# An RWKV layer with two mixtures of experts: lone slots by column parts, the ranking in three portions, the last tiles' routing reordered

## The chip, the core and the metric

One core of one Trainium2 chip runs the whole kernel in one launch. The metric is the device time of one execution in microseconds (us), lower is better. A run counts with its own time. The profile belongs to one execution, and its times count from that execution's first instruction.

## The reference

Three stages follow each other: a linear attention with a decaying state, a first mixture whose eight experts all see all 1536 rows, and a second mixture that sends each row to one expert.

```python
# attention: B, H, S, D = 2, 8, 768, 48
for t in range(S):
    cur = einsum('bhd,bhe->bhde', u * k[t], v[t])
    y[t] = einsum('bhd,bhde->bhe', r[t], state + cur)
    state = w[t][..., None] * state + einsum('bhd,bhe->bhde', k[t], v[t])
x = y as 1536 rows of 384
# first mixture: 8 experts, 384 -> 1024 -> 384, all rows
P = 8 rounds of row and column scaling of exp(x @ w_gate - max)
x = sum over e of P[:, e] * (relu(x @ w1[e]) @ w2[e])
# second mixture: top 1
logits = normed(x) @ normed(expert_emb).T / tau
idx = argmax(logits); gate = softmax(logits)[idx]
out[row] = gate[row] * (relu(x[row] @ w1[idx]) @ w2[idx])
```

## The kernel before

The rows are 12 tiles of 128. TensorE does nearly all the work in products that take each operand as a high and a low part (three matmuls for one product), and the order of the whole program is written out by hand: a unit of work is a list of pieces, `run` issues a piece and then the side items that stand at its place in a second list. An engine executes its instructions in that order.

The last expert of the first mixture runs in four units of three tiles (`m1_unit(E - 1, ...)`). A unit has 8 hidden pieces (`h_piece`, L274, one per 128 hidden columns) and then the output pieces (`y_part`, L294 to L296), after which VectorE adds the tile to `acc` (`m1_finish`, L804). Beside the units run the steps of the second mixture's routing for tiles that are ready: `route_dots` (products with the embeddings, two thirds on VectorE at L731, one third on GpSimd at L738 and ScalarE at L724), `route_arg` (the choice), `gate_a` (an inverse norm, 13 small instructions on VectorE or 16 on GpSimd, L817 to L832), `route_pos` and `route_cum` (the row's place among its expert's rows), `gate_b`, `gate_c` (the softmax weight, L988), and `route_rows`, a scatter by GpSimd of each row to its place in the buffer `xs` (L958). Tiles 10 and 11 take `route_tr` and `route_mm` in place of the dots: three transposes (L893) and twelve small matmuls.

After the counts of the first tiles `choose` picks the expert that slot 0 will run, and after 8 tiles `order` ranks the other seven by their counts (23 small VectorE instructions, L1012 to L1049): slots 3, 5 and 7 (`TURN`, the lone slots) get the three smallest.

The second mixture is a sequence of ten slots (`m2_slot`). A slot loads its up to 256 rows from `xs` (`m2_load`, on SyncE's queue, behind all scatters so far), transposes and splits them (`m2_xT`, L707 to L712: TensorE, ScalarE, VectorE), and runs one expert. The expert's weights arrive in seven pieces in six stage buffers; each is split into a high part by ScalarE (L252) and a low part by VectorE (L258), which then lets SyncE load the next. Slot 0 computes both halves of 128 rows, a later slot its second half only under `tc.If`, by a bit of a word that is computed in slot 1.

A normal slot has 8 hidden pieces for 256 rows at once and 2 output pieces for each half. A lone slot works on one half (`turned_pieces` with `own=True`): three slabs accumulate x times the 1024 hidden columns in three PSUM banks, with the rows stationary; then ScalarE takes the relu of each bank (`hid`, L335); three `turn` steps transpose it into a bank of their own (L341), ScalarE writes the high part `hh` (L344) and VectorE the low part `hl` (L345); then come four output pieces. Its list has ten pieces: slab, slab, slab, turn, turn, turn, y, y, y, y.

Where side items stand is a table of numbers in `m2_slot`:

```python
if turned:
    its = its[KD:]
    at_ = (0, 1, 3, 5)
...
else:
    at_ = (5, 6, 7, 8, 9, 15, 15) if s == 0 else (1, 4, 6, KF, KF, KF + 1, KF + 1)
```

PSUM has eight banks, and `ps()` hands them out in turn. GpSimd's queue carries its arithmetic, the scatters and the output scatters in one order; SyncE's carries all loads in one order.

Of the kernel before, what the change touches and what calls it, by code (L numbers as in the profile page):

```python
# [19 lines left out]
def rwkv_sinkhorn_moe_top1_moe(  # L20
# [974 lines left out]
    def choose():  # L995
# [9 lines left out]
        nc.vector.tensor_scalar(oe, wdesc, m, None, op0=ALU.is_equal)  # L1005

    def order():
# [8 lines left out]
        nc.vector.tensor_scalar(mk, kio, est[:, 0:1], full, op0=ALU.is_ge, op1=ALU.mult)  # L1016
        b = small[0].tile([128, NS], F32, tag="b", name="b")
        nc.vector.tensor_tensor(b, kio, mk, ALU.add)
        nc.vector.tensor_scalar(ids[:, E - 1:E], est[:, 0:1], 0.0, None, op0=ALU.add)
        nf = sp.tile([128, E], F32, tag="fl", name="nf")  # L1020
        nc.vector.tensor_scalar(nf[:, 0:1], full, -1.0, 1.0, op0=ALU.mult, op1=ALU.add)
# [5 lines left out]
        key = sp.tile([128, E], F32, tag="jk", name="key")
        nc.vector.scalar_tensor_tensor(out=key, in0=p, scalar=float(E), in1=wdesc, op0=ALU.mult, op1=ALU.add)
        nc.vector.scalar_tensor_tensor(out=key, in0=oe, scalar=float(OOB), in1=key, op0=ALU.mult, op1=ALU.add)
        sq = [128, E, E]  # L1030
        c = sp.tile([128, NTILE, E], F32, tag="tmp", name="rank")[:, 0:E]
        nc.vector.tensor_tensor(
            c, key.unsqueeze(1).to_broadcast(sq), key.unsqueeze(2).to_broadcast(sq), ALU.is_gt
        )
        nc.vector.tensor_reduce(f, c, axis=AX.X, op=ALU.add)
        se = [128, E - 1, E]
        d = c[:, 0:E - 1]
        c = sp.tile([128, NTILE, E], F32, tag="tl", name="at")[:, 0:E - 1]
        nc.vector.tensor_tensor(
            c, f.unsqueeze(1).to_broadcast(se), want.unsqueeze(2).to_broadcast(se), ALU.is_equal  # L1040
        )
        nc.vector.tensor_tensor(d, c, wdesc.unsqueeze(1).to_broadcast(se), ALU.mult)
        nc.vector.tensor_reduce(b[:, 1:E], d, axis=AX.X, op=ALU.add)
        nc.vector.tensor_scalar(b[:, 1:E], b[:, 1:E], -1.0, float(E), op0=ALU.mult, op1=ALU.add)
# [495 lines left out]
```

## Time and profile before

| | |
|---|---|
| time, median of 3 runs | 1045.87 us (1043.79 to 1046.72) |
| the profiled execution's own time | 1045.61 us |
| its span, first to last instruction | 1043.9 us |
| PE (matmul) busy | 1015.2 us, 97% |
| DVE, ACT, POOL busy | 700.9, 413.9, 207.1 us |
| mean granted TensorE clock | 0.993 of full |
| moved by DMA | 91.71 MB, 85.60 MB of it through SyncE's queue |

PE is TensorE's matmuls, DVE is VectorE, ACT is ScalarE, POOL is GpSimd and SP is SyncE. The first mixture's last expert runs from about 780 us to 870, slot 0 from 870 to 892.6, the three lone slots from 928.0, 957.6 and 987.2, and the last matmul stands at 1034.1. A row of a timeline has the start, the duration, the engine, the line, the operation, what it writes and reads, and, in brackets, how long the engine had been idle and what ended that. Matmuls overlap, so the spacing of their starts tells how fast they go.

### The profile page before, as it was taken

Reading aid. Unit: us, or ns where it says so; the run is one execution under the profiler, and the core shown is the slowest. Engines: PE = TensorE matmul, PEld = TensorE weight load, DVE = VectorE, ACT = ScalarE, POOL = GpSimd, SP = SyncE. Lnnn points to the kernel's source line nnn. Section 1 sums busy time; section 2 is a strip of 40 time slices with the busy share of each in tenths; the row PEclk is TensorE's granted clock in tenths of the full one; section 3 lists DMA queues with packets and bytes.
Section 4 is the critical chain, followed back from the end, with each engine's and each line's share of the span. In section 5 each row is a group of like instructions: output and inputs, shape, how many; then the busy total and the mean of one; then the engine's idle time right before and its main releaser. Section 6 shows DMA issues by size and latency. Waiting matters only on the chain.

```text
span 1043.9 us, 19767 instructions
## 1 busy us (share of the span) xinstructions
PE 1015.2 (97%) x7714; PEld 995.0 (95%) x7714; DVE 700.9 (67%) x1413; ACT 413.9 (40%) x851; POOL 207.1 (20%) x393
## 2 busy tenths in 40 slices
PE   7999999999999999999999999999999998999996
PEld 6899999999999999999999999999999997999996
DVE  7998858666655665566456556655547787977764
ACT  3323234535432342333234323433434545566553
POOL 3211152040100010002001000000234663144101
PEclk9999999999999999999999999999999999999998
DMA  8435201201220122021011100120011314888762
GB/s 248 120 109 158 84 10 46 76 1 31 84 78 1 61 84 77 10 88 50 7 31 61 31 1 31 61 77 15 19 59 37 100 38 139 293 300 281 244 207 68
DMA packets 55783, 91.71 MB, mean 88 GB/s; under 512 B 5355, under 2 KB 47191, under 8 KB 55554
## 3 DMA queue, kind: packets, MB, share of 16 engines
q1 hardware_dynamic: 53056, 85.60, 26.4%
q0 software_dynamic: 2624, 4.75, 1.2%
q8 instruction: 64, 1.05, 0.4%
q14 instruction: 37, 0.30, 0.1%
q10 hardware_dynamic: 2, 0.00, 0.0%
HBM read 80.42 MB, written 13.28 MB: 90 GB/s over the span
## 4 chain that ended last, share of the span: by engine, by line
PE 67%; issue 14%; DVE 9%; POOL 5%; ACT 2%; DMA 1%; POOLq 0%; DVEq 0%; SPq 0%; ACTq 0%
PE ps L502 29%; PE ps L427 24%; PE ps L274 6%; PE ps L294 2%; PE ps L296 2%; PE ps L295 1%; POOL tmp L738 1%; DVE ps L731 1%; POOL xs L1136 1%; PE ps L631 1%; POOL out_dram L1182 1%; DVE hl L443 1%; DVE keep L438 1%; PE ps L663 1%; ACT hh L442 1%
## 5 line engine op out<-in xcount | busy, mean ns | idle before, releaser
L502 PE MATMUL ps<-wA,hh 128*128 128x384 f32 x864 | 221.6, 337 | 0.4 <-ACT hh L442 0.4
L502 PEld LDWEIGHTS ps<-wA,hh 128*128 128x128 f32 x864 | 156.7, 188 | 1.2 <-ACT hh L442 1.2
L506 DVE SCALAR_TENSOR_TENSOR acc<-ps,Pe,acc 128x384 f32<-128x384 f32 x144 | 88.7, 616 | 101.7 <-PE ps L502 101.3
L433 ACT ACTIVATE keep<-ps 128x384 f32<-128x384 f32 x144 | 70.2, 488 | 208.9 <-PE ps L427 207.1
L502 PE MATMUL ps<-wA,hl 128*128 128x384 f32 x432 | 145.6, 337 | 0.2
L443 DVE SCALAR_TENSOR_TENSOR hl<-keep,hh 128x384 fp32r<-128x384 f32 x144 | 81.7, 567 | 92.0 <-ACT hh L442 92.0
L438 DVE TENSOR_TENSOR keep<-ps,keep 128x384 f32<-128x384 f32 x192 | 106.3, 554 | 40.2 <-PE ps L427 34.2
L232 POOL TENSOR_TENSOR stage<-stage 128x128 f32<-128x128 f32 x96 | 49.3, 535 | 416.4 <-DMA stage<-in_moe_w_dram 414.5
L442 ACT ACTIVATE hh<-keep 128x384 fp32r<-128x384 f32 x144 | 75.4, 524 | 123.8 <-DVE keep L438 123.6
L427 PE MATMUL ps<-xTAhi,wA 128*128 128x384 f32 x396 | 101.6, 338 | 0.2 <-ACT keep L433 0.2
L279 ACT ACTIVATE hh<-ps 128x256 fp32r<-128x256 f32 (+1 forms) x128 | 53.0, 416 | 91.5 <-PE ps L274 72.9
L294 PE MATMUL ps<-wA,hh 128*128 128x384 f32 x248 | 85.1, 343 | 1.8 <-ACT hh L344 1.7
L296 PE MATMUL ps<-wA,hl 128*128 128x384 f32 x248 | 83.6, 337 | 0.4
L295 PE MATMUL ps<-wA,hh 128*128 128x384 f32 x248 | 83.3, 336 | 0.0
L502 PEld LDWEIGHTS ps<-wA,hl 128*128 128x128 f32 x432 | 81.1, 188 | 1.2 <-DVE hl L443 1.2
L258 DVE TENSOR_TENSOR wA<-stage,wA 128x768 fp32r<-128x768 f32 (+2 forms) x65 | 72.5, 1118 | 4.9 <-ACT wA L252 4.6
L280 DVE SCALAR_TENSOR_TENSOR hl<-ps,hh 128x256 fp32r<-128x256 f32 (+1 forms) x128 | 57.5, 460 | 26.6 <-ACT hh L279 26.2
L502 PE MATMUL ps<-slot,hh 128*128 128x384 f32 x288 | 74.2, 339 | 0.0
L427 PEld LDWEIGHTS ps<-xTAhi,wA 128*128 128x128 f32 x396 | 71.7, 188 | 0.5 <-ACT keep L433 0.5
L252 ACT ACTIVATE wA<-stage 128x768 fp32r<-128x768 f32 (+2 forms) x65 | 60.5, 956 | 26.6 <-POOL stage L232 26.0
L427 PE MATMUL ps<-xTAlo,wA 128*128 128x384 f32 x198 | 66.7, 337 | 0.0
L274 PE MATMUL ps<-xTAhi,wA 128*128 128x256 f32 (+1 forms) x336 | 58.3, 309 | 0.0
(332 smaller groups left out, 2093.1 us busy)
## 6 DMA issues: line engine op xcount, KB each, us to landing
stage<-in_moe_w_dram SPq DMA_DIRECT2D x55, 384.0 KB
stage<-in_moe_w_dram SPq DMA_DIRECT2D x19, 512.0 KB
en<-in_moe_w_dram SPq DMA_DIRECT2D x17, 512.0 KB
stage<-in_moe_w_dram SPq DMA_DIRECT2D x28, 256.0 KB
rkv<-in_rkv_dram SPq DMA_DIRECT2D x12, 576.0 KB
en<-in_moe_w_dram SPq DMA_DIRECT2D x18, 384.0 KB
rk<-in_wrk_dram SPq DMA_DIRECT2D x24, 192.0 KB
stage<-in_moe_w_dram SPq DMA_DIRECT2D x28, 128.0 KB
```

The source lines that it names most:

```text
L258: eng.tensor_tensor(out=lo, in0=src, in1=hi.bitcast(F32), op=ALU.subtract)
L274: nc.tensor.matmul(p[:, 0:n], w1_of(g, kk, f)[lo], b[:, kk, :], start=(i == 0), stop=(i == len(mm) - 1))
L294: nc.tensor.matmul(p, hh[:, ts], w2h, start=(f == 0), stop=False)
L295: nc.tensor.matmul(p, hh[:, ts], w2l, start=False, stop=False)
L296: nc.tensor.matmul(p, hl[:, ts], w2h, start=False, stop=(f == KF - 1))
L427: nc.tensor.matmul(t, w, x, start=first_mm and q == 0, stop=q == n - 1, skip_group_check=True,)
L433: nc.scalar.activation(out=t, in_=st_[i][bank][:, 0:384], func=AF.Copy)
L438: nc.vector.tensor_tensor(t, st_[i][bank][:, 0:384], t, ALU.add)
L442: nc.scalar.activation(out=hh, in_=src, func=AF.Relu)
L443: nc.vector.scalar_tensor_tensor(out=hl, in0=src, scalar=0.0, in1=hh.bitcast(F32), op0=ALU.max, op1=ALU.subtract)
L502: nc.tensor.matmul(p, h[:, ts], w, start=n == 0, stop=n == len(mm) - 1)
L506: nc.vector.scalar_tensor_tensor(out=a, in0=p, scalar=P[:, t, e:e + 1], in1=a, op0=ALU.mult, op1=ALU.add)
```

## The change

The lone slot's three slabs become three parts: a part does all nine matmuls of its columns in one bank, and its transposes are written back into that bank. The list is now part 0, part 1, turn 0, part 2, turn 1, y, turn 2, y, y, y. The next slot's rows are transposed after the first y piece (place 5 in place of 2), two of the slot's four weight splits stand ahead of its first piece and two at places 2 and 6.

`order` loses its ranking. `rank_a`, `rank_b` and `rank_c` do it one unit earlier, with the counts of 6 tiles; what `order` keeps is ten instructions. `choose` gains two. In the third unit tile 3 to 5's scatters stand behind tile 6's products, and a split moves forward. In the fourth unit a split of slot 0's weights leaves for slot 0, and two thirds of tile 9's dots move behind the next output. In slot 0 the inverse norm of tiles 10 and 11 goes from VectorE to GpSimd and is asked for earlier, the scatters of tiles 8 and 9 stand directly ahead of those of 10 and 11, and the five splits of slot 1's weights move from places 5 to 9 to places 8 to 12. The condition of `tc.If` takes one register operation less.

```diff
-                    hid.append(hp.tile([128, 384], F32, tag="hh", name="hid") if own else acc[:, 8 + i])
+                    hid.append(acc[:, 8 + i])
...
+        def part(i):
+            p, fs = ps(), parts[i]
+            n = len(fs) * 128
+            cs = slice(fs[0] * 128, fs[0] * 128 + n)
+            mm = [(a, b, kk) for a, b in ((xh, w1h), (xh, w1l), (xl, w1h)) for kk in range(KD)]
+            for q, (a, b, kk) in enumerate(mm):
+                nc.tensor.matmul(p[:, 0:n], a[:, kk, :], b[:, kk, cs], start=(q == 0), stop=(q == len(mm) - 1))
+            hid.append(hp.tile([128, 384], F32, tag="hh", name="hid"))
+            nc.scalar.activation(out=hid[i][:, 0:n], in_=p[:, 0:n], func=AF.Relu)
+            banks.append(p)
...
-            t, n = ps(), len(parts[i]) * 128
+            t, n = banks[i] if own else ps(), len(parts[i]) * 128
...
+            return [pa[0], pa[1], ts[0], pa[2], ts[1], ys[0], ts[2]] + ys[1:]
...
+    def rank_a():
+        p = counts()
+        key = rr["key"] = small[0].tile([128, E], F32, tag="sc1", name="key")
+        nc.vector.scalar_tensor_tensor(out=key, in0=p, scalar=float(E), in1=mk[:, 0:E], op0=ALU.mult, op1=ALU.add)
...
+    def rank_b():
...
+        nc.vector.tensor_scalar(blk[:, 1:E], mk[:, 1:E], -1.0, float(E), op0=ALU.mult, op1=ALU.add)
+
+    def rank_c():
...
+        nc.vector.tensor_reduce(wtab, a.rearrange("p s e -> p e s"), axis=AX.X, op=ALU.add)
+        nc.vector.tensor_scalar_add(mk[:, 0:1], est[:, 0:1], -float(E - 1))
...
-                side[2].append(lambda: m2_xT(s + 1))
+                side[5 if turned else 2].append(lambda: m2_xT(s + 1))
...
-                its = its[KD:]
-                at_ = (0, 1, 3, 5)
+                its, pre = its[KD + 2:], its[KD:KD + 2]
+                at_ = (2, 6)
...
-                at_ = (5, 6, 7, 8, 9, 15, 15) if s == 0 else (1, 4, 6, KF, KF, KF + 1, KF + 1)
+                at_ = (8, 9, 10, 11, 12, 15, 15) if s == 0 else (1, 4, 6, KF, KF, KF + 1, KF + 1)
...
-            with tc.If(((word[0] >> s) & 1) > 0):
+            with tc.If((word[0] & (1 << s)) > 0):
...
-            dt[0:1], dt[1:2], dt[2:3], rt[0:2], its[1:2], [], [rt[2]], [rt[3]],
-            its[2:3], rt[4:], dots_of(6), its[3:4], dots_of(7), its[4:5],
+            dt[0:1], dt[1:2], dt[2:3], rt[0:2], its[1:2], its[2:3], [rt[2]], [rt[3]],
+            [rank_a, rt[4], rank_b], [rank_c], dots_of(6), its[3:4] + [rt[5]], dots_of(7), its[4:5],
...
-        ra, rb = route(8, 10, nc.gpsimd), route(10, 12, nc.vector)
+        ra, rb = route(8, 10, nc.gpsimd), route(10, 12, nc.gpsimd)
...
-            [order, lambda: load_to(E + SURE)], its[5:6], [], [], dots_of(9)[0:2], dots_of(9)[2:], [ra[1]], [ra[0]],
-            [], [lambda: m2_xT(0)], [lambda: route_tr(10)], [ra[2], ra[3]],
+            [order, lambda: load_to(E + SURE)], [], [], [], dots_of(9)[0:1], [], [], dots_of(9)[1:] + [ra[1], ra[0]],
+            [], [lambda: m2_xT(0)], [lambda: route_tr(10)], [lambda: sumsq(11), ra[2], ra[3]],
...
-            (0, [lambda: route_mm(10), lambda: route_tr(11), ra[4], more_stages]), (1, [lambda: route_mm(11), ra[5], rb[0], rb[1]] + its[6:7]),
-            (3, rb[2:4]), (4, rb[4:]), (5, [lambda: m2_load(1)]), (6, [lambda: m2_load(2)]),
-            (10, [overflow]), (14, [lambda: m2_xT(1)]),
+            (0, [lambda: route_mm(10), lambda: route_tr(11), ra[4], rb[1], more_stages]),
+            (1, [lambda: route_mm(11)]), (2, rb[0:1]), (3, its[5:6]), (4, rb[2:4]+[ra[5]]+rb[4:] + [lambda: m2_load(1)]), (5, its[6:7]+[lambda: m2_load(2)]), 
+            (8, [overflow]), (14, [lambda: m2_xT(1)]),
```

How this moves instructions, at three places. The rows name an instruction by its line (the changed kernel has its own line numbers), its operation, and what it writes and reads.

First DVE in the fourth unit, at the end of `order`: `wtab` is its last result, `wB` a low part of slot 0's weights, `acc` a tile's sum, `lg` a dot. Before:

```order
L1047 TENSOR_REDUCE wtab<-at 128x8
L1048 TENSOR_SCALAR nf<-nf 128x1
L1049 SCALAR_TENSOR_TENSOR wtab<-oe,nf,wtab 128x8
L258 TENSOR_TENSOR wB<-stage_66,wB 128x768
L804 SCALAR_TENSOR_TENSOR acc<-ps,Pe,acc 128x384
L731 ISA ps,lg<-ps,en 128x384
L731 ISA lg 128x1
```

Of the change:

```order
L1078 TENSOR_SCALAR sc_9536<-sc_9536 128x1
L1079 SCALAR_TENSOR_TENSOR wtab<-oe,sc_9536,wtab 128x8
L819 SCALAR_TENSOR_TENSOR acc<-ps,Pe,acc 128x384
L746 ISA ps,lg<-ps,en 128x384
L746 ISA lg 128x1
L746 ISA ps,lg<-ps,en 128x384
L746 ISA lg 128x1
L819 SCALAR_TENSOR_TENSOR acc<-ps,Pe,acc 128x384
```

The split ahead of tile 9's sum is gone, and tile 10's sum now stands behind two dots; before, five dots came ahead of it.

Then DVE from the end of `overflow` in slot 0 to the rows of slot 1 (`wA` are low parts of slot 1's weights, `o` an output half, `slo` the low part of slot 1's rows). Before:

```order
L1074 TENSOR_TENSOR oex<-d,ids 128x6
L1180 TENSOR_SCALAR o<-ps,rows_9309 128x384
L712 TENSOR_TENSOR slo_9315<-ps,shi_9313 128x3x128 x2
L1180 TENSOR_SCALAR o<-ps,rows_9309 128x384
L258 TENSOR_TENSOR wA<-stage_64,wA 128x768
```

Of the change:

```order
L1104 TENSOR_TENSOR oex<-d,ids 128x6
L258 TENSOR_TENSOR wA<-stage_65,wA 128x1024
L258 TENSOR_TENSOR wA<-en,wA 128x1024 x2
L1210 TENSOR_SCALAR o<-ps,rows_9325 128x384
L258 TENSOR_TENSOR wA<-en,wA 128x768
L258 TENSOR_TENSOR wA<-stage_66,wA 128x768
L727 TENSOR_TENSOR slo_9331<-ps,shi_9329 128x3x128 x2
L1210 TENSOR_SCALAR o<-ps,rows_9325 128x384
```

Five splits that stood ahead of `overflow`'s ten instructions now stand behind them, directly ahead of `slo`.

Last PE in slot 3, a lone slot; the number behind `ps` tells one PSUM tile from another. Before, from the last of the 27 matmuls that make the hidden columns:

```order
L327 MATMUL ps_10627<-wA_70,slo1_9315 128x384
L327 MATMUL ps_10628<-wA_70,slo1_9315 128x384
L327 MATMUL ps_10629<-wA_70,slo1_9315 128x256
L707 MATMUL ps_10679<-ident_76,rows0_9309 128x128 x3
L707 MATMUL ps_10685<-ident_76,rows0_9309 128x128 x3
L341 MATMUL ps_10691<-ident_76,hid_10673 128x128 x3
L341 MATMUL ps_10705<-ident_76,hid_10675 128x128 x3
L341 MATMUL ps_10713<-ident_76,hid_10677 128x128 x2
L294 MATMUL ps_10726<-wA_70,hh_10695 128x384
L295 MATMUL ps_10726<-wA_70,hh_10695 128x384
L296 MATMUL ps_10726<-wA_70,hl_10696 128x384
```

Of the change, from the first of them:

```order
L343 MATMUL ps_10616<-wA_70,shi1_9329 128x384 x6
L343 MATMUL ps_10616<-wA_70,slo1_9331 128x384 x3
L343 MATMUL ps_10638<-wA_70,shi1_9329 128x384 x6
L343 MATMUL ps_10638<-wA_70,slo1_9331 128x384 x3
L352 MATMUL ps_10616<-ident_76,hid_10626 128x128 x3
L343 MATMUL ps_10660<-wA_70,shi1_9329 128x256 x6
L343 MATMUL ps_10660<-wA_70,slo1_9331 128x256 x3
L352 MATMUL ps_10638<-ident_76,hid_10648 128x128 x3
L294 MATMUL ps_10682<-wA_70,hh_10653 128x384
L295 MATMUL ps_10682<-wA_70,hh_10653 128x384
L296 MATMUL ps_10682<-wA_70,hl_10654 128x384
```

A part's matmuls now stand between another part's relu and its transposes, and the transposes go to the bank that held the part, so a half takes four PSUM tiles where it took seven.

## Rows read from the trace of the kernel before

**Rows 1.** The page: busy time, share of the span and instructions of each engine.

```profile
PE 1015.2 (97%) x7714; PEld 995.0 (95%) x7714; DVE 700.9 (67%) x1413; ACT 413.9 (40%) x851; POOL 207.1 (20%) x393
```

**Rows 2.** PE's waits from 800 us to the end: us in total, times, longest.

```profile
PE ps L893 <- DVE acc L804: 2.8, 1, 2.8
PE ps L274 <- DVEq L1397: 2.1, 3, 0.7
PE ps L294 <- ACT hh L344: 1.7, 3, 0.6
PE ps L274 <- DVE lg L731: 0.7, 1, 0.7
PE ps L296 <- DVE hl L280: 0.7, 1, 0.7
PE ps L707 <- DMA rows<-xs: 0.4, 1, 0.4
```

**Rows 3.** A stretch: length, busy us of PE, PEld, DVE, ACT, POOL, clock, DMA, GB/s.

```profile
865.00:875.00 10.00, 7.19 (x65) 6.16 (x63) 7.38 (x33) 5.39 (x18) 5.94 (x19) 0.83 0.53 176
```

**Rows 4.** Timeline of DVE in the fourth unit, from `order` to tile 10's sum.

```profile
856.37 0.15 DVE L1012 TENSOR_TENSOR sc<-ps,oe 128x8 f32<-128x8 f32 x1
...
861.83 0.95 DVE L258 TENSOR_TENSOR wB<-stage,wB 128x768 fp32r<-128x768 f32 x1
...
864.40 0.57 DVE L731 CUSTOM_DVE_ANT_0 ps<-ps,en 128x384 f32<-128x384 f32 x1 [1.10 <-ACT ps L877]
...
867.52 0.61 DVE L804 SCALAR_TENSOR_TENSOR acc<-ps,Pe,acc 128x384 f32<-128x384 f32 x1
```

**Rows 5.** Timeline of DVE ahead of the fourth unit.

```profile
840.11 1.34 DVE L258 TENSOR_TENSOR wB<-stage,wB 128x768 fp32r<-128x768 f32 x1 [3.04 <-ACT wB L252]
```

**Rows 6.** A stretch from tile 11's end to slot 1's rows, columns as in rows 3.

```profile
869.94:893.07 23.13, 22.03 (x174) 20.53 (x174) 18.98 (x73) 10.72 (x23) 5.63 (x11) 0.94 0.38 121
```

**Rows 7.** Timeline of DVE in slot 0: the inverse norm's first of 13, and the split behind it.

```profile
876.57 0.16 DVE L817 TENSOR_SCALAR ssq<-ssq 128x2 f32<-128x2 f32 x1
...
879.01 0.96 DVE L258 TENSOR_TENSOR wB<-stage,wB 128x768 fp32r<-128x768 f32 x1
```

**Rows 8.** Timeline of PE in slot 3, a lone slot, and into slot 4.

```profile
928.00 1.10 PE L327 MATMUL ps<-wA,shi 128*128 128x384 f32 x6
...
932.20 0.82 PE L707 MATMUL ps<-ident,rows 128*128 128x128 f32 x6
932.86 1.04 PE L341 MATMUL ps<-ident,hid 128*128 128x128 f32 x8
934.46 0.44 PE L294 MATMUL ps<-wA,hh 128*128 128x384 f32 x1 [0.57 <-ACT hh L344]
...
935.50 0.34 PE L294 MATMUL ps<-wA,hh 128*128 128x384 f32 x1
...
938.97 0.34 PE L296 MATMUL ps<-wA,hl 128*128 128x384 f32 x1
940.02 0.98 PE L274 MATMUL ps<-shi,wB 128*128 128x256 f32 x6 [0.71 <-DVEq L1397]
```

**Rows 9.** Timelines of ACT and of DVE in slot 3.

```profile
933.88 0.53 ACT L344 ACTIVATE hh<-ps 128x384 fp32r<-128x384 f32 x1
934.25 0.89 ACT L252 ACTIVATE wB<-en 128x768 fp32r<-128x768 f32 x1
934.62 0.55 DVE L345 TENSOR_TENSOR hl<-ps,hh 128x384 fp32r<-128x384 f32 x1
```

**Rows 10.** Timeline of ACT ahead of slot 5, the next lone slot.

```profile
952.90 1.06 ACT L252 ACTIVATE wB<-stage 128x1024 fp32r<-128x1024 f32 x1 [1.32 <-DMA stage<-in_moe_w_dram]
```

**Rows 11.** Timeline of DVE and POOL in the third unit.

```profile
824.83 0.20 POOL L827 TENSOR_TENSOR nrm_a<-nrm_y 128x3 f32<-128x3 f32 x1
...
825.04 1.22 DVE L258 TENSOR_TENSOR wB<-stage,wB 128x1024 fp32r<-128x1024 f32 x1
825.10 1.21 POOL L828 TENSOR_TENSOR nrm_a<-nrm_a,ssq 128x3 f32<-128x3 f32 x1
```

More of the change, by code (lines that the diff above doesn't have):

```diff
@@ L348, in turn @@
                 hts.append((hh[:, cs], hl[:, cs]))
-        return [lambda k=k: slab(k) for k in range(KD)] + [lambda i=i: turn(i) for i in range(3)] + [
-            lambda q=q: y_part(g, q, 4, 0, hts, box) for q in range(3)
-        ] + [lambda: finish(0, y_part(g, 3, 4, 0, hts, box))]
+        ys = [lambda q=q: y_part(g, q, 4, 0, hts, box) for q in range(3)]
+        ys.append(lambda: finish(0, y_part(g, 3, 4, 0, hts, box)))
+        ts = [lambda i=i: turn(i) for i in range(3)]
+        if own:
+            pa = [lambda i=i: part(i) for i in range(3)]
+            return [pa[0], pa[1], ts[0], pa[2], ts[1], ys[0], ts[2]] + ys[1:]
+        return [lambda k=k: slab(k) for k in range(KD)] + ts + ys
     S_t = {}
@@ L895, in route_tr @@
         nc.scalar.activation(out=xT, in_=tp[:, 0:DM], func=AF.Copy)
-        sumsq(t)
+        if t < NTILE - 1:
+            sumsq(t)
         rr[t] = xT
@@ L935, in route_pos, with route_idx @@
                 nc.tensor.matmul(pb[:, i, :], a, b, start=(q == 0), stop=(q == len(mm) - 1))
+        rr["pb", t0] = pb
+    def route_idx(t0, t1):
+        n = t1 - t0
+        ts = slice(t0, t1)
+        pb = rr.pop(("pb", t0))
         lm = small[0].tile([128, n], F32, tag=f"lm{n}", name="lm")
@@ L1015, in order @@
         nc.vector.tensor_single_scalar(full, full, float(CAP), op=ALU.is_ge)
[L1016 to L1021, printed above, removed]
@@ L1022, in order @@
-        nc.vector.tensor_scalar_add(nf[:, 1:2], est[:, 0:1], -float(E - 1))
+        nc.vector.tensor_scalar(f[:, 0:1], full, -1.0, 1.0, op0=ALU.mult, op1=ALU.add)
+        b = small[0].tile([128, NS - E], F32, tag="b", name="b")
+        nc.vector.tensor_scalar(mk[:, E:NS], kio[:, E:NS], est[:, 0:1], full, op0=ALU.is_ge, op1=ALU.mult)
+        nc.vector.tensor_tensor(b, kio[:, E:NS], mk[:, E:NS], ALU.add)
         nc.vector.scalar_tensor_tensor(
-            out=b[:, E:E + 1], in0=nf[:, 1:2], scalar=nf[:, 0:1], in1=b[:, E:E + 1], op0=ALU.mult, op1=ALU.add
+            out=b[:, 0:1], in0=mk[:, 0:1], scalar=f[:, 0:1], in1=b[:, 0:1], op0=ALU.mult, op1=ALU.add
@@ L1025, in order @@
         )
[L1027 to L1044, printed above, removed]
@@ L1045, in order @@
-        nc.vector.tensor_scalar_min(blk, b, float(E + NOV - 1))
-        nc.vector.tensor_tensor(c, c, pow2.unsqueeze(2).to_broadcast(se), ALU.mult)
-        nc.vector.tensor_reduce(wtab, c.rearrange("p s e -> p e s"), axis=AX.X, op=ALU.add)
-        nc.vector.tensor_scalar_mul(nf[:, 0:1], nf[:, 0:1], float(1 << E))
-        nc.vector.scalar_tensor_tensor(out=wtab, in0=oe, scalar=nf[:, 0:1], in1=wtab, op0=ALU.mult, op1=ALU.add)
+        nc.vector.tensor_scalar_min(blk[:, E:NS], b, float(E + NOV - 1))
@@ L1051, in overflow @@
+        nc.vector.tensor_scalar_mul(f[:, 0:1], f[:, 0:1], float(1 << E))
+        nc.vector.scalar_tensor_tensor(out=wtab, in0=oe, scalar=f[:, 0:1], in1=wtab, op0=ALU.mult, op1=ALU.add)
     def overflow():
@@ L1343, in route @@
                 lambda: gate_a(t0, t1, eng),
-                lambda: (route_pos(t0, t1), route_cum(t0, t1)),
+                lambda: (route_pos(t0, t1), route_cum(t0, t1), route_idx(t0, t1)),
                 lambda: gate_b(t0, t1),
@@ L1363, in m2_slot @@
             its = w_items(E + s + 1)
-            turned = s in TURN
+            turned, pre = s in TURN, []
             side = [[] for _ in range(KF + 8)]
@@ L1393, in m2_slot @@
             n = 10 if turned else KF + 2
+            for it in pre:
+                it()
             run(pieces[:n], side)
```

20 lines of the change are left out of this document (added).

## The prediction

> **What bounds the kernel now.** I read the page first: PE is busy 97% of the span [rows 1]. Only time in which PE waits, or runs at the lower clock, can come back from a change that keeps every matmul, and the change touches nothing ahead of about 820 us. So the second view is PE's waits from 800 us on [rows 2]: six rows with 8.4 us in all, and the change goes at each. The third is the granted clock: 0.83 over 865 to 875 [rows 3], which is the only dip to the 1.2 GHz level in this half of the kernel. Then come the timelines at these places, where the starts of matmuls tell more than the idle figures, since a modelled matmul end hides part of a wait.
>
> **The change part by part.** The sum is made against the profiled execution, 1045.6 us by its own time; the median of the runs stands 0.3 above it.
>
> *Tile 10's sum, fourth unit.* PE waits 2.8 us for it, the longest of the six [rows 2]. VectorE comes late: `order` takes it from 856.37 to 861.83, the split of slot 0's weights 0.95, then five dots from 864.40 to 867.52, and only then the sum [rows 4]. `order` keeps 10 of 23 instructions; at the stretch's mean (5.46 / 23 = 0.24 us) that frees 3.1, the split 0.9, and three dots of 0.62 now stand behind the sum (1.9). That is 5.9 us ahead of a sum that is 2.8 late, so the wait goes with some 3 us to spare: **-2.8**. The removed ranking lands in the third unit, 14 instructions or 3.4 us at the same mean. It is paid at nothing because VectorE stands idle there for 3.04 us at one place alone [rows 5]; without that cover it would push the dots of tiles 6 and 7 back by 3.4.
>
> *The clock.* The dip begins after this wait: PE is idle 2.8 us, and then the granted clock is at half for (1 - 0.83) x 2 x 10 = 3.4 us [rows 3], in which PE does 1.7 us of work less. The waits that I expect to stay are near 1 us, and the lone slots' waits of up to 0.9 have no dip behind them. So it goes with the wait: **-1.7**.
>
> *Scatters behind products, third unit.* The 0.7 us for `lg` [rows 2] come from dots of tile 7 that started late: VectorE idled 3.04 us for a split of ScalarE's [rows 5], which stood behind sums of GpSimd's products, which stood behind three scatters. With the products first, the 3 us shrink and the dots are over before PE wants their bank: **-0.7**. The scatters' own lateness is covered by a whole unit, for `m2_load(0)` waits for later ones.
>
> *Slot 0.* Here VectorE and PE end together today: from tile 11's last matmul to the low part of slot 1's rows 23.1 us pass [rows 6]. For PE 1.4 of these are clock (0.06 x 23.1), 0.7 the wait for `hl`, 0.4 the wait for the rows [rows 2, 6], so its own need is 20.6. VectorE loses the inverse norm's 13 instructions (876.57 to 879.01, 2.4) and gains a split (0.9) [rows 7, 4]: 23.1 - 2.4 + 0.9 = 21.6, with its other pauses as they are. The weight splits, moved from ahead of `overflow` to behind it, still stand ahead of `slo`, so nothing in this sum leaves; they only stop delaying `hl`. VectorE's 21.6 then sets the end, and a new wait of about 1 us for `slo` opens at slot 1's first piece. The old waits go, and of 23.1 only **-1.5** is left, the larger part (1.4) being clock that I have counted: beyond the clock it is 0.1. Its bounds are PE's need, -2.5, and nothing at all if VectorE's pauses grow by 1.5. I take VectorE's figure, since its queue is the fuller by the row. The scatters: GpSimd now does both inverse norms, then four scatters in a row; tile 11's squares are there before its choice, so the norm is off the chain, and the rows come 1 to 2 us earlier against a need 2 us earlier, within what `slo` hides.
>
> *Lone slots.* Slot 3 goes from 928.00 to 940.02, 12.0 us [rows 8]. Its matmuls need 4.20 (27 hidden, to 932.20), 0.66 (six transposes), 0.88 (eight more at 0.11) and 24 x 0.1735 = 4.16 (20 of them from 935.50 to 938.97), together 9.9. The 2.1 that are lost lie at two places. From the transposes' end (933.74) to 935.50, 1.24 us go on waiting for `hh` and `hl`, 0.53 and 0.55 long, with a split of 0.89 between [rows 9]. At the end, 0.88 lies between 939.14 and 940.02, for VectorE (DVEq in the row) still reads the bank that slot 4's first piece gets. With parts, the relu (as long as `hh`, 0.53) lies beside another part's 1.56, `hh` and `hl` (1.08) beside part 2 (1.08) and turn 1 (0.33) with 0.35 more until the first matmul that reads `hl`; a half takes three banks fewer, so slot 4's first piece gets another bank and in the built program waits for VectorE no more. Three lone slots ran one half each (the rows at slot ends stand three times in rows 2). I leave 0.1 for hand-offs: 3 x 2.0 = **-6.0**. The splits ahead of the slot cost nothing while ScalarE is free and their weights are there; without that, up to 0.89 each. One register operation less per branch is nothing, because at the normal slots' branches PE shows no wait [rows 2].
>
> Sum: 2.8 + 1.7 + 0.7 + 0.1 + 6.0 = 11.3, from 1045.6 to 1034.3, and 0.3 for the median: **1034.6 us**.
>
> Against this stands a rule of the Trainium skill (SBUF — State Buffer, "Who interferes with whom"): a VectorE instruction with two SBUF inputs and a GpSimd instruction that reads SBUF exclude each other, and the later one stands still for the other's whole length. The change puts 16 dependent GpSimd instructions beside VectorE's routing. The trace agrees in one row: a GpSimd instruction of 0.20 us took 1.21 beside a split of 1.22 [rows 11]. By the row, the price here is one such hit, 1.0, on a chain with as much to spare, so the sum stays; the rival below takes the rule at its worst.
>
> **The rivals.** *The lone slots give half back* (0.12). ScalarE waits 1.32 us for weights just ahead of slot 5 [rows 10]; lone slots that are 2 us shorter leave the loads less time, and two splits now stand ahead of the relu that PE waits for. Against it: the normal slot in which the loads are busiest keeps its length. If 1.0 of each 2.0 returns, 1037.6.
>
> *The wait moves to slot 0's end* (0.13). If VectorE's stretch doesn't shorten by the norm, since it waits for GpSimd instead, it is 24.0 against PE's 20.6: a wait of 3.4, longer than the one that had the dip behind it, so another 1.7 of clock: 20.6 + 3.4 + 1.7 = 25.7 for 23.1, 2.6 more where I had 1.5 less: 1038.7. For it speaks that rows 6 leave VectorE no 3 us of slack; against it that the norm's inputs are there early.
>
> *GpSimd's chain crawls: slower* (0.03). If each of the 16 instructions of the norm takes 1.21 in place of 0.20, slot 1's rows come 16 us late; 1 is hidden behind `slo`, PE idles 15 more and loses 1.7 of clock: 1051.3. It decides from a mean of about 1.0 us: 13 us more than the chain's slack, less than which the change still wins. Against it: only a split was long enough to hold one so, and none stands beside the chain's start.
>
> *The ranking is another one* (0.02). If six tiles' counts put an expert of over 128 rows in a lone slot, a second half of 9.9 us runs: 1044.5, no change to be seen. I counted the choices with the reference on the inputs: after 6 and after 8 tiles the order is the same, and the lone experts end with 18, 28 and 83 rows.
>
> **How the numbers follow.** The forecast has 0.70. The range goes from 1032.2 (slot 0 at PE's own need, the lone slots without remainder, and the hidden 0.2 of the small waits) to 1039.6, which takes in the first two rivals with 0.9 for a single hit in each; 0.05 lies above it and some below. A measurement of this kernel tells 0.3% (3 us) from no change. Faster by more: the forecast and the first two rivals, 0.95 less a little for what I don't see, 0.94. Within: 0.03. Slower: 0.03.
>
> **What would show it.** Right: no PE wait for `acc` over 0.5 us in the fourth unit and a clock of 1.00 there; lone slots of 9.9 to 10.1 from first matmul to the next slot's; PE's longest wait of the second mixture about 1 us, for `slo`, at slot 1's first piece. Wrong: a dip of the clock near slot 0's end, ScalarE waiting for weights inside a lone slot, GpSimd instructions of the norm near 1 us, or a second half in slot 3, 5 or 7.

## The result and the profile after

The changed kernel takes 1036.73 us (median of 4 runs, 1035.24 to 1038.07), the kernel before 1045.13 in the same runs: a ratio of 0.992 with an interval of 0.990 to 0.994, so 8.4 us less where 11.3 were predicted. The forecast was 1034.6 with a range of 1032.2 to 1039.6. The profiled execution took 1038.07, its span is 1036.4.

The page's first part and PE's waits from 800 us on (columns as in [rows 1, 2]):

```profile
PE 1013.5 (98%) x7715; PEld 994.3 (96%) x7715; DVE 700.6 (68%) x1400; ACT 414.9 (40%) x851; POOL 210.6 (20%) x409
```

```profile
PE ps L274 <- DVE slo L727: 0.7, 1, 0.7
PE ps L296 <- DVE hl L280: 0.5, 1, 0.5
PE ps L294 <- PE ps L296: 0.4, 1, 0.4
PE ps L274 <- PEq L1429: 0.3, 2, 0.2
PE ps L722 <- DMA rows<-xs: 0.2, 1, 0.2
```

The 8.4 us of [rows 2] are down to 2.1, most of them in new waits. The first mixture's last expert starts at 762.5 in the kernel before, not at about 780 as was said ahead; its second unit starts at 788.03. The changed kernel's execution is 1.64 us late there (789.67 us), and that is not the change's: up to there both kernels do the same, yet that unit's first matmul starts anywhere from 787.8 to 789.7 over the fourteen profiles of this study. One reason shows in the windows of 15 to 45 us, of the kernel before and of the changed one, where the granted clock differs:

```profile
15.00:45.00 30.00, 23.43 (x436) 20.29 (x437) 28.80 (x49) 10.78 (x23) 9.52 (x6) 0.94 0.60 169
```

```profile
15.00:45.00 30.00, 22.90 (x393) 19.50 (x392) 27.81 (x46) 9.99 (x20) 8.64 (x6) 0.89 0.69 176
```

So stages are compared by their lengths, each from its first matmul to the next stage's in PE's timeline, and the whole from the second unit's start to the end of the span. In us:

| | third unit | fourth unit | slot 0 | slot 1 | slot 2 | slots 3+5+7 | slots 4+6+8 | second unit to end |
|---|---|---|---|---|---|---|---|---|
| before | 25.65 | 31.01 | 22.39 | 17.95 | 17.48 | 36.07 | 52.60 | 255.87 |
| changed | 25.86 | 26.65 | 20.11 | 20.55 | 17.62 | 30.71 | 53.27 | 246.69 |
| e1_slabs | 25.85 | 26.65 | 20.01 | 20.21 | 17.61 | 36.09 | 53.16 | 251.95 |
| e7_parts | 25.65 | 31.85 | 21.25 | 18.09 | 17.48 | 30.73 | 53.08 | 250.08 |
| e2_at59 | 25.85 | 26.65 | 20.80 | 21.06 | 18.19 | 30.66 | 53.19 | 248.61 |
| e3_its5 | 25.87 | 26.65 | 19.92 | 20.72 | 18.22 | 30.65 | 53.10 | 247.11 |
| e4_rbvec | 25.87 | 26.65 | 20.71 | 20.03 | 17.61 | 30.70 | 53.16 | 246.71 |
| e6_noif | 25.87 | 26.65 | 19.88 | 20.50 | 19.02 | 29.84 | 53.40 | 247.33 |
| e8_load2 | 25.84 | 26.65 | 19.93 | 18.97 | 18.95 | 30.75 | 53.29 | 246.42 |
| e9_pool6 | 25.85 | 26.65 | 20.10 | 19.52 | 18.25 | 30.68 | 53.29 | 246.58 |
| e11_over | 25.85 | 26.65 | 20.04 | 18.83 | 17.61 | 30.71 | 53.07 | 245.19 |
| e12_pool | 25.84 | 26.65 | 20.08 | 19.56 | 17.62 | 30.67 | 53.09 | 246.15 |
| e13_oact | 25.87 | 26.65 | 20.01 | 18.93 | 17.61 | 30.70 | 53.10 | 245.18 |

The changed kernel, e1_slabs and e6_noif are the same program up to slot 2, and their slots 0 and 1 together took 40.66, 40.22 and 40.38: a difference of less than 0.45 there tells nothing. By this measure the change wins 9.2 us, of which 0.86 lie behind the last matmul, a stretch that takes 8.9 to 9.8 us in these profiles whatever the kernel.

**The fourth unit.** DVE's sum for tile 10, PE's transposes of it, and the window of [rows 3]:

```profile
862.90 0.61 DVE L819 SCALAR_TENSOR_TENSOR acc<-ps,Pe,acc 128x384 f32<-128x384 f32 x1
```

```profile
866.09 0.49 PE L908 MATMUL ps<-ident,acc 128*128 128x128 f32 x3
```

```profile
865.00:875.00 10.00, 10.00 (x104) 9.45 (x103) 6.92 (x34) 5.24 (x15) 6.42 (x31) 1.00 0.40 142
```

The sum ends at 863.51, 2.6 us ahead of its use; there is no wait, and the clock stays at the 2.4 GHz level.

**Slots 0 and 1.** PE, then VectorE, ScalarE and SyncE of the changed kernel, from slot 1's first piece to its output pieces:

```profile
889.32 0.62 PE L274 MATMUL ps<-slo,wA 128*128 128x256 f32 x3 [0.66 <-DVE slo L727]
...
903.23 0.44 PE L296 MATMUL ps<-wA,hl 128*128 128x384 f32 x1 [0.48 <-DVE hl L280]
904.06 0.43 PE L294 MATMUL ps<-wA,hh 128*128 128x384 f32 x1 [0.39 <-PE ps L296]
```

```profile
892.35 0.96 DVE L258 TENSOR_TENSOR wA<-stage,wA 128x768 fp32r<-128x768 f32 x1 [1.70 <-ACT wA L252]
```

```profile
891.47 0.85 ACT L252 ACTIVATE wA<-stage 128x768 fp32r<-128x768 f32 x1 [2.70 <-DMA stage<-in_moe_w_dram]
```

```profile
882.79 0.38 SPq L1183 DMA_DIRECT2D rows<-xs  x1
883.75 0.38 SPq L215 DMA_DIRECT2D stage<-in_moe_w_dram  x1
884.94 0.38 SPq L1183 DMA_DIRECT2D rows<-xs  x1
885.57 0.37 SPq L215 DMA_DIRECT2D stage<-in_moe_w_dram  x1
```

The wait for `slo` is the forecast one (0.82 from start to start). The other two, 0.64 and 0.66 from start to start, are new. Of these only the first is for `hl`. At the second the row names PE itself: in the trace PE's sequencer starts to load the word for `tc.If` at 903.22, when the late `hl` releases it, and branches at 903.91, so the late `hl` lays this bare. The origin of both is the last weight piece of slot 1. It is asked for at 885.57, behind the rows of slots 1 and 2, and ScalarE gets it 5.9 us later. VectorE stands 1.70 for its split, and the rest of what VectorE has to do in slot 1 stands behind it. Slot 1 grew by 2.60, slot 0 lost 2.28.

**Lone slots.** PE in slot 3, answering to [rows 8]:

```profile
925.96 1.21 PE L343 MATMUL ps<-wA,shi 128*128 128x384 f32 x6
...
935.69 0.34 PE L296 MATMUL ps<-wA,hl 128*128 128x384 f32 x1
936.18 0.95 PE L274 MATMUL ps<-shi,wB 128*128 128x256 f32 x6 [0.15 <-PEq L1429]
```

10.22 us in place of 12.02. Of the last spacing, 0.49, a matmul of this width takes 0.17; the rest ends with PE's sequencer at the `tc.If`.

### The profile page after: what moved, and what is told of

The parts are those of the page before. It is cut to its first block, busy times and chain, and to the rows that moved or that the text cites. A ratio compares the mean times of both kernels' runs of the same rounds, so it can differ in the third digit from the quotient of the medians.

```text
span 1036.4 us, 19729 instructions
## 1 busy us (share of the span) xinstructions
PE 1013.5 (98%) x7715; PEld 994.3 (96%) x7715; DVE 700.6 (68%) x1400; ACT 414.9 (40%) x851; POOL 210.6 (20%) x409
## 4 chain that ended last, share of the span: by engine, by line
PE 73%; issue 8%; DVE 8%; DMA 5%; POOL 3%; ACT 2%; SPq 0%; POOLq 0%; DVEq 0%; ACTq 0%
PE ps L517 29%; PE ps L442 25%; PE ps L274 8%; DMA xs<-acc,oidx 4%; PE ps L294 3%; PE ps L296 2%; PE ps L295 2%; DMA stage<-in_moe_w_dram 2%; POOL out_dram L1212 1%; PE ps L646 1%; DVE ps L746 1%; DVE hl L458 1%; DVE keep L453 1%; POOL xs L1166 1%; PE ps L678 1%
```

## The experiments

**The lone slots by themselves.** e1_slabs is the changed kernel with the slabs back (and with them the places of the rows and of the splits):

```diff
-            t, n = banks[i] if own else ps(), len(parts[i]) * 128
+            t, n = ps(), len(parts[i]) * 128
...
-        if own:
-            pa = [lambda i=i: part(i) for i in range(3)]
-            return [pa[0], pa[1], ts[0], pa[2], ts[1], ys[0], ts[2]] + ys[1:]
```

> The changed kernel with its lone slots as before: slabs, transposes in banks of their own, the next slot's rows at place 2, the four weight splits at places 0, 1, 3 and 5. In the changed kernel a lone slot took 10.22 to 10.27 us and slots 4, 6 and 8 took 17.69 to 17.89, against 12.02 and 17.5 before. Theory (the parts are worth 1.8 per lone slot whatever stands ahead of them): slots 3, 5 and 7 at 12.0 again, the rest as in the changed kernel, 5 us longer from slot 3's start to the last matmul. Rival (the longer slots 4, 6 and 8 and the shorter lone slots are two sides of the loads): slots 4, 6 and 8 go back to 17.5, so that only 4.7 return. Slots 0 and 1 (20.1 and 20.55) stay in either case.

1043.07 us against 1047.8 for the kernel before on the same chip. The lone slots are back at 36.09, slots 4, 6 and 8 stay at 53.2: the theory. e7_parts is the other way round, the kernel before with this half of the change alone:

> The kernel before with the lone-slot part of the change alone (parts, transposes in the parts' banks, the order of pieces, rows at place 5, two splits ahead of the slot). Theory (the two halves of the change don't touch each other): lone slots 10.2, slots 4, 6 and 8 17.7 or so, 4.7 less in all, and everything up to slot 2 as in the kernel before (fourth unit 31.0, slots 0 and 1 40.3). Rival (the routing half made room for them): lone slots of 11 or more.

1040.04 against 1046.78, lone slots 30.73: the theory again. The stages up to slot 2 are as before within 0.2 in sum but not one by one: the fourth unit took 0.84 more and slot 0 1.14 less, since more of the clock's dip lies ahead of slot 0 (a granted clock of 0.54 over 868 to 870, 0.81 in the kernel before). Without the tail behind the last matmul, the two halves give 5.0 (e7_parts) and 3.5 (e1_slabs) of the 8.3 us; they add up. In every kernel with either half, slots 4, 6 and 8 take 0.5 to 0.8 more than before; with the halves apart the loss doesn't split, and its cause stays open.

**The skip.** e6_noif leaves the second halves of lone slots out:

```diff
+            if turned:
+                return
             with tc.If((word[0] & (1 << s)) > 0):
```

> The changed kernel without the conditional second halves of the three lone slots (128 rows fewer can be served there; the branch, its skip and the skipped code are gone). Theory (the 0.32 us that PE still loses at a lone slot's end, of which 0.09 is an ordinary change of form, is the skip: a taken branch of 0.35 to 0.39 and a semaphore behind the last matmul): slots 3, 5 and 7 take 10.0 in place of 10.22 to 10.27, 0.7 in all. Rival (the bank or the split of slot 4's rows ends the lone slot): they stay at 10.2. Slots 0 and 1 as in the changed kernel, 40.7 together.

Slots 3, 5 and 7 take 9.97, 9.93 and 9.94: the skipped block costs 0.29 each. By the trace it is rather the wait behind it than the branch: in the changed kernel's trace the branch of slot 3 has ended at 935.49, ahead of the last matmul's start at 935.69, and what PE's sequencer does last, at 936.07, stands behind that matmul's signal, which lands at 936.04. The runs don't separate the two. In PE's timeline of this run the next slot follows at a matmul's own pace:

```profile
935.07 0.34 PE L296 MATMUL ps<-wA,hl 128*128 128x384 f32 x1
935.24 0.87 PE L274 MATMUL ps<-shi,wB 128*128 128x256 f32 x6
```

The whole was no faster (1036.89), since slot 2, which is the same program in both, took 19.02 in this execution. That led to e11_over below.

**Is VectorE slot 0's bound?** Three edits of its queue:

```diff
@@ e2_at59
-                at_ = (8, 9, 10, 11, 12, 15, 15) if s == 0 else (1, 4, 6, KF, KF, KF + 1, KF + 1)
+                at_ = (5, 6, 7, 8, 9, 15, 15) if s == 0 else (1, 4, 6, KF, KF, KF + 1, KF + 1)
@@ e3_its5
-            [order, lambda: load_to(E + SURE)], [], [], [],
+            [order, lambda: load_to(E + SURE)], its[5:6], [], [],
@@ e4_rbvec
-        ra, rb = route(8, 10, nc.gpsimd), route(10, 12, nc.gpsimd)
+        ra, rb = route(8, 10, nc.gpsimd), route(10, 12, nc.vector)
```

> The changed kernel with the five splits of slot 1's weights in slot 0 at places 5 to 9 in place of 8 to 12. Theory (VectorE's queue as a whole is the bound through slots 0 and 1, and the order within it moves nothing): slots 0 and 1 together stay at 40.7 us within 0.4; a wait for hl may come back in slot 0's output pieces and that for slo at slot 1's start shrink by as much. Rival (slot 1's late waits come from the last weight piece, whose load stands behind the first of these splits): VectorE's pause of 1.70 us ahead of that piece's split shrinks by 1 or more, slot 1's two waits for hl (0.64 and 0.66) go, and slots 0 and 1 take 39.5.

> The changed kernel with the split of slot 0's sixth weight piece back in the fourth unit, ahead of tile 9's sum. Tile 10's sum ended 2.6 us ahead of its use, so 0.95 more ahead of it opens no wait there under either theory. Theory (VectorE's work between tile 11's last sum and slot 1's rows sets slot 0's end, 0.95 less of it): the wait for slo (0.82) goes; the loads that stand behind this split are issued 13 us earlier, the last piece lands earlier, and slot 1's waits for hl shrink too: slots 0 and 1 together 39.3 in place of 40.7. Rival (the rows' arrival sets slot 0's end): the wait for slo turns into one for the rows, and slots 0 and 1 lose 0.3 at most.

> The changed kernel with the inverse norm of tiles 10 and 11 back on VectorE (13 instructions, 2.4 us) at its new place. Theory (VectorE is the bound of slot 0): slot 1's first piece waits 2.4 us more for slo (3.2), slots 0 and 1 together 43.1, and 1.7 us more if the clock dips behind such a wait. Rival (GpSimd's chain, its scatters and the rows' load set that end): the scatters come earlier, the wait for the rows goes, and slots 0 and 1 change by less than 0.5.

Neither 2.4 us more work on VectorE (e4_rbvec, 1036.2 us, slots 0 and 1 40.74 together against 40.66) nor 0.95 less (e3_its5, 1037.36 us, 40.64) moved the sum: by the sum the theory fell twice. But the sum hides what happened in slot 0. VectorE starts on `slo` 20.57 to 20.60 behind slot 0's first matmul in the seven kernels with the change's queue there, 21.02 in e4_rbvec and 20.15 in e3_its5: 2.4 us more moved it by 0.43, 0.95 less by 0.44. Why by so little shows in VectorE's pauses in slot 0, of the changed kernel and of e4_rbvec:

```profile
870.22 0.43 DVE L280 SCALAR_TENSOR_TENSOR hl<-ps,hh 128x256 fp32r<-128x256 f32 x1 [0.62 <-ACT hh L279]
...
873.13 0.42 DVE L280 SCALAR_TENSOR_TENSOR hl<-ps,hh 128x256 fp32r<-128x256 f32 x1 [1.21 <-ACT hh L279]
```

```profile
868.34 0.42 DVE L280 SCALAR_TENSOR_TENSOR hl<-ps,hh 128x256 fp32r<-128x256 f32 x1 [0.62 <-ACT hh L279]
...
876.58 0.17 DVE L1008 TENSOR_REDUCE es<-ex 128x2 f32<-128x16 f32 x1 [0.34 <-ACT ex L1002]
```

The pause of 1.21 is gone there: work placed early in slot 0 falls into pauses. In e3_its5 a new pause of 0.44 ahead of an `hl` takes up half of what left. e2_at59 (1038.91 us) met neither expectation: 41.86, 1.2 worse. The wait for `slo` fell from 0.82 to 0.20, as the splits that stand directly ahead of it were done, but a wait for `hl` of 0.76 came back in slot 0, and slot 1 kept 0.64 and 0.66 and gained one of 1.14. So the places 8 to 12 of the change are worth 1.2.

What sets the sum of the two slots is the last weight piece of slot 1. VectorE's split of it, of e2_at59, of e3_its5 and of e4_rbvec:

```profile
892.45 0.96 DVE L258 TENSOR_TENSOR wA<-stage,wA 128x768 fp32r<-128x768 f32 x1 [2.79 <-ACT wA L252]
```

```profile
891.24 0.96 DVE L258 TENSOR_TENSOR wA<-stage,wA 128x768 fp32r<-128x768 f32 x1 [2.12 <-ACT wA L252]
```

```profile
890.51 0.96 DVE L258 TENSOR_TENSOR wA<-stage,wA 128x768 fp32r<-128x768 f32 x1 [1.29 <-ACT wA L252]
```

Counted from slot 0's first matmul these are 25.87, 24.68 and 24.71; in the changed kernel it is 24.68, in e1_slabs 24.22, in e6_noif 24.36. In all six slot 1 ends 15.96 to 16.03 behind that start. So these edits were measured behind a later limit: what they did to slot 0 could not show in the sum, and e2_at59 lost its 1.2 because SyncE asked for the piece 0.9 later and it came 1.2 later.

**The late weight piece.** e8_load2 asks for slot 2's rows later; e9_pool6 takes the piece's low part from VectorE:

```diff
@@ e8_load2
-            (5, its[6:7]+[lambda: m2_load(2)]), (8, [overflow]),
+            (5, its[6:7]), (8, [overflow]), (9, [lambda: m2_load(2)]),
@@ e9_pool6
-        lambda j=j: split_piece(g, j, lo_engine)
+        lambda j=j: split_piece(g, j, nc.gpsimd if g == E + 1 and j in (6,) else lo_engine)
```

> The changed kernel with one load moved: the rows of slot 2 are asked for behind the first split of slot 1's weights, so that the load of slot 1's last weight piece stands ahead of them on SyncE. Theory (slots 0 and 1 are bound by that piece's arrival: VectorE stands 1.70 us for it and is late from there to slot 1's output pieces): the piece is issued 1.2 earlier and lands 1.2 to 2 earlier, VectorE's pause shrinks by as much, PE's two waits of 0.64 and 0.66 for hl in slot 1 shrink by 1 us together, slots 0 and 1 take 39.5 in place of 40.7. Rival (VectorE's own work is the bound): the pause goes but the waits for hl stay, within 0.3 of 40.7. Second rival (the loads run at all the bandwidth there is): the piece lands when it did, since the loads behind it take what the rows leave.

> The changed kernel with the low part of slot 1's last weight piece made by GpSimd in place of VectorE (about twice 1.04 us, by its products over 384 columns). Theory (VectorE's order puts slot 1's hidden low parts behind a piece that lands late): VectorE neither stands 1.70 for the piece nor spends 0.96 on it, both waits for hl go, slots 0 and 1 take 39.3 in place of 40.7; the wait for slo (0.82) stays, for it lies ahead. Rival (PE is held in slot 1 by the weights themselves or by VectorE's other work): less than 0.5 is won.

In e8_load2 ScalarE's split of the last piece:

```profile
887.29 0.85 ACT L252 ACTIVATE wA<-stage 128x768 fp32r<-128x768 f32 x1 [0.20 <-DMA stage<-in_moe_w_dram]
```

That execution is 1.51 us earlier at the second unit, so the piece is there 2.7 us earlier than in the changed kernel. VectorE has no pause for the piece in slot 1, both waits in slot 1's output pieces are gone, slots 0 and 1 take 38.90: 1.8 us less, the theory and more. e9_pool6 gives 39.62, somewhat less than expected, as one of the two waits stays at 0.66. But neither kernel was faster as a whole (1036.28 and 1036.47 us), for slot 2 took 18.95 and 18.25. ScalarE and GpSimd there, in e8_load2:

```profile
910.63 0.49 ACT L724 ACTIVATE shi<-ps 128x384 fp32r<-128x384 f32 x1 [1.00 <-PE ps L274]
912.86 0.39 ACT L279 ACTIVATE hh<-ps 128x256 fp32r<-128x256 f32 x1 [1.74 <-PE ps L274]
```

```profile
910.05 1.16 POOL L1166 DMA_INDIRECT xs<-acc,oidx  x1 [0.30 <-issue]
911.51 0.97 POOL L1166 DMA_INDIRECT xs<-acc,oidx  x1 [0.30 <-issue]
```

By their rows the matmuls that ScalarE reads were long done (the last of the piece read at 912.86 starts at 909.83 and ends by 910.2). But the trace also records TensorE's signals (semaphore updates). That of this piece lands at 912.84, 3.0 us behind the matmul's start, ScalarE starts 0.02 behind it, and the next two signals follow in steps of 0.1; in e11_over a signal lands 0.29 behind its matmul's start. So ScalarE did wait for TensorE, and what is late is the signal. The longest such pause of ScalarE is in e6_noif:

```profile
914.13 0.39 ACT L279 ACTIVATE hh<-ps 128x256 fp32r<-128x256 f32 x1 [2.51 <-PE ps L274]
```

e11_over takes the scatters out of slot 2:

```diff
-            if 2 <= s <= 5:
-                for i, j in enumerate((3, 5, 7)):
-                    side[j].append(lambda t=3 * (s - 2) + i: over_scatter(t))
+            if 3 <= s <= 5:
+                for i, j in enumerate((1, 3, 5, 7)):
+                    side[j].append(lambda t=4 * (s - 3) + i: over_scatter(t))
```

> The kernel of e8_load2 with the overflow scatters of slot 2 moved: four each in slots 3, 4 and 5 in place of three each in slots 2 to 5. In e8_load2 slot 1 won 1.6 us and slot 2 lost 1.3 (18.95 against 17.62): ScalarE stood 1.00 and 1.74 us there, ended by nothing that its inputs explain, beside two of these scatters of GpSimd's. Theory (ScalarE stands still beside the software scatters): without them slot 2 takes 17.5, slots 0 and 1 stay at 38.9, and from the second unit to the end the time is 1.4 less than e8_load2's 246.4, unless slots 3 to 5 lose it. Rival (slot 2 is held by VectorE's work carried over from slot 1): slot 2 stays at 18.5 or more.

Slot 2 takes 17.61, slots 0 and 1 38.86, and the whole 245.19: the theory's numbers, and 1.5 below the changed kernel. In the four profiles with the scatters moved slot 2 takes 17.61 or 17.62 and no signal of TensorE is late there; in the ten with them it takes 17.48 to 19.02 (17.62 or less in five) and signals are late in each.

That the scatters are the cause isn't shown, for the chip changed with them. e1_slabs to e9_pool6 ran on one chip, the four later kernels on two others; for the kernel before and the changed one the record names none. Two places speak for the chip. In slot 0 e8_load2 and e11_over are the same program, with scatters at the same offsets, and the signal of the piece beside the second scatter lands 0.62 behind its matmul's start in e8_load2 (0.63 in the changed kernel) and 0.29 in the four. And in slot 4, where scatters stand in all fourteen, three of e11_over's four at the changed kernel's offsets within 0.06, ScalarE stands still in the changed kernel and not in e11_over:

```profile
942.96 0.38 ACT L279 ACTIVATE hh<-ps 128x256 fp32r<-128x256 f32 x1 [1.83 <-PE ps L274]
```

In the four, slot 4 takes 17.69 or 17.70, in the changed kernel 17.89. So scatters seem to go with late signals on one chip and not on two others; e8_load2 on one of those would tell, and no run here is that.

**What is left in slots 0 and 1.** e12_pool gives two low parts to GpSimd, e13_oact the output halves of slots 0 and 1 to ScalarE, both on top of e11_over:

```diff
@@ e12_pool
-        lambda j=j: split_piece(g, j, lo_engine)
+        lambda j=j: split_piece(g, j, nc.gpsimd if (g, j) in ((E + 1, 4), (E + 2, 2)) else lo_engine)
@@ e13_oact
-            nc.vector.tensor_scalar_mul(o, p, rows[:, tl, DM:DM + 1])
+            if s < 2:
+                nc.scalar.activation(out=o, in_=p, func=AF.Copy, scale=rows[:, tl, DM:DM + 1])
+            else:
+                nc.vector.tensor_scalar_mul(o, p, rows[:, tl, DM:DM + 1])
```

> The kernel of e11_over with two low parts made by GpSimd in place of VectorE: the fifth weight piece of slot 1 (in slot 0, behind the scatters and ahead of slot 1's rows) and the third of slot 2 (in slot 1). VectorE has 19.0 us of work in slot 1 and no pause, PE needs 17.5. Theory (VectorE's work is what is left of the bound in slots 0 and 1): the wait for slo at slot 1's start (0.8 to 1.0) goes with the first, slot 1 takes 17.8 with the second, slots 0 and 1 together 37.3. Rival (VectorE stands still beside GpSimd's longer instructions on the same memory): no gain, and VectorE's splits beside them take over 1.5 in place of 1.2.

> The kernel of e11_over with the four weighted output halves of slots 0 and 1 made by ScalarE in place of VectorE (0.53 us of VectorE's queue each, one of them ahead of slot 1's rows; ScalarE stands idle over 2 us at these places). Theory (VectorE's work is what is left of the bound in slots 0 and 1; 18.8 us in slot 1 against PE's 17.5): the wait for slo at slot 1's start falls from 0.89 to 0.4 or less, slot 1 takes 17.8 or less in place of 18.83, slots 0 and 1 together 37.8 in place of 38.9, and the whole is 1 us below e11_over. Rival (the rows' arrival and the way over the transposes and ScalarE set slot 1's start, and VectorE's later work is hidden): slots 0 and 1 stay within 0.3 of 38.9.

e12_pool: 1036.51 us (4 runs, ratio 0.991, 0.990 to 0.993). The wait for `slo` went, as the theory has it, but slots 0 and 1 take 39.64, no gain: the rival. GpSimd and VectorE at the second of the parts:

```profile
896.34 2.42 POOL L258 TENSOR_TENSOR wB<-en,wB 128x1024 fp32r<-128x1024 f32 x1 [0.25 <-ACT wB L252]
```

```profile
897.07 2.78 DVE L258 TENSOR_TENSOR wB<-en,wB 128x1024 fp32r<-128x1024 f32 x1
```

VectorE's split of 1.22 took 2.78: it ended 1.09 after GpSimd's, so it stood 1.56 of the 1.69 that were left of that one, and PE then waited 1.45 for `hl`. This is the rule of the Trainium skill (SBUF — State Buffer, "Who interferes with whom") by which a VectorE instruction with two inputs from SBUF and a GpSimd instruction that reads SBUF exclude each other, the later one standing still until the other ends; here the trace agrees.

e13_oact: 1034.86 us (5 runs, ratio 0.990, 0.988 to 0.991). The wait for `slo` fell to 0.41, as expected, and a wait of 0.66 at slot 1's output (the word and the branch again) came in its place, 38.94 in all: the rival's number, though not by the rival's way. Its median lies 0.3 below that of e14_over5, and the runs overlap. e14_over5 is e11_over in rounds:

> The kernel of e11_over again, timed in rounds. From the second unit's start to the end it was 1.5 us below the changed kernel in one profile (245.19 against 246.69), so 1035.2 is expected where the changed kernel's median is 1036.7 and the kernel before 1045.9; if slot 1's late weight piece and the scatters were a matter of one execution, it is 1036.7.

1035.16 us (1034.42 to 1035.72, 5 runs, ratio 0.990, 0.988 to 0.992), from the second unit to the end 244.86. It expected 1035.2. The kernel before took 1045.70 beside it, 10.5 more. The changed kernel wasn't timed beside it; its four runs have a median of 1036.73 and overlap at the edge, so how much of the 1.6 is the moved load's, the scatters' or the chip's is open.

## Why the prediction was right, and where not

The forecast was right in its sign, its range and most of its terms. Point by point:

- *Tile 10's sum, the clock, `lg`*: right. Third and fourth unit and slot 0 together lost 6.4 us, of which 0.82 came back as the forecast wait for `slo`; 5.6 stands against 5.3 (2.8, 1.7, 0.7 and 0.1). The sum's margin was 2.6 for "some 3". With no long wait there was no dip. The ranking, "paid at nothing", stands in a third unit that is 0.2 longer in every kernel that has it there.
- *Slot 0, VectorE's 21.6 sets the end*: VectorE does set it, and the wait for `slo` at slot 1's first piece came at its forecast size; by the prediction's own measure the 21.6 are 21.7 (867.49 to 889.19). But the working behind the number was wrong, and that it came out is luck: the norm counted as 2.4 is worth 0.43 of `slo`'s time (e4_rbvec), the split counted as 0.9 is worth 0.44 (e3_its5), so the two cancel, and the fall from 23.1 has another source, which no run isolates. The phrase that failed is "with its other pauses as they are": VectorE's early pauses take in what is added there. Work directly ahead of `slo` counts in full: 0.53 less (e13_oact) brought it 0.51 earlier than in e11_over, 0.95 less (e12_pool) 0.87.
- *What the account left out: slot 1.* It ended at slot 1's first piece. Slot 1's last weight piece waits on SyncE behind the rows of slots 1 and 2, and VectorE's timeline has no pause in slot 1's 17.95 us already in the kernel before. So a piece that VectorE waits 1.7 us for shows in full: slot 1 grew by 1.8 beyond the wait for `slo`. e8_load2 shows it by one moved load, and the 16.0 us from that piece's split to slot 1's end in six kernels say the same. I had asked what the loads do ahead of the lone slots, and not here, where the slot ahead of them got shorter.
- *Lone slots, -6.0*: the mechanism is right, the size was off by 0.6: 5.36, slots of 10.22 to 10.27 where 9.9 to 10.1 were to be seen. I left 0.1 for each slot's hand-offs; the skipped block takes 0.29 (e6_noif). Before, it lay under the 0.88 that PE waited for VectorE's bank, so no row showed it alone; the normal slots' branches, which I took as the measure, run their second half and skip nothing.
- *Slots 4, 6 and 8*: not forecast, 0.67 longer in sum. The spacings of slot 4's 48 output matmuls sum to 8.64 us, to 8.34 before; 0.2 of slot 4 go with the late signal there, since it takes 17.69 or 17.70 in the four kernels without one. For the rest the cause is open.
- *The range*: its lower end doesn't follow from the terms named for it. PE's own need in slot 0 is 1.0 more, the lone slots without remainder 0.3, the small waits 0.2: that gives 1033.1, not 1032.2. The measured time lies far from either.

By terms, -5.6, +1.8, +0.1 (slot 2), -5.4 and +0.7 make -8.4, about what the medians show. With the tail's 0.9 that is the table's 9.2, and the late start of the profiled execution takes 1.6 off: 7.5, from 1045.6 to 1038.1.

The rivals: the lone slots gave nothing back by late weights, though weights were late one stage earlier; no dip came at slot 0's end; GpSimd's norm of tiles 10 and 11 took 0.19 to 0.23 us an instruction, but no split of VectorE's stood beside its chain, so the rule was hardly put to the test there. In the changed kernel's third unit two instructions of an earlier norm took 1.21 and 1.24 beside splits, as in [rows 11], and e12_pool has the rule at full size. No second half ran.

```profile
870.04 0.20 POOL L842 TENSOR_TENSOR nrm_a<-nrm_y 128x2 f32<-128x2 f32 x1
```

```profile
826.74 1.21 POOL L843 TENSOR_TENSOR nrm_a<-nrm_a,ssq 128x3 f32<-128x3 f32 x1
```

## What to carry to other kernels

When a stage gets shorter, follow the account one stage further on: the loads that it used to cover, and the queue of the engine that had no pause there. An engine's work in a stage counts only in part while there are pauses behind it; look at what stands in its queue between an input's arrival and the result that is waited for. Before a sum over stages is read as "no effect", look whether a later arrival sets that sum. When an edit and the chip change together, a place where the program is the same tells them apart. A wait that is removed may have covered a smaller one, and a row for an uncovered case of the same kind is needed to price it.

## What was not expected of the hardware

Signals of TensorE's matmuls landed up to 3.0 us behind the start of the matmul (0.29 as a rule, e11_over), and ScalarE stood idle up to 2.51 us for them (e6_noif), beside GpSimd's indirect scatters. It is not the same each time: the changed kernel and e6_noif are the same program up to slot 2, and it took 17.62 and 19.02 there. In the four profiles of two other chips no signal is late beside a scatter, not even where the program is the same. Whether it is the chip, the scatters on that chip or something else was not tried. And a skipped `tc.If` costs 0.29 us of PE's time at a lone slot's end, where by the trace PE's sequencer waits for PE's own signal ahead of the next matmuls.
